# Diagonal of the score tiles by one predicated copy from the third block on, eight buffers for the streamed low halves, and a new table of due times

## The chip, the cores and the metric

The kernel runs on one core of a Trainium2 chip. TensorE (PE) multiplies matrices into eight PSUM banks; VectorE (DVE), ScalarE (ACT) and GpSimd (POOL) work on the elements; SyncE (SP) issues every DMA. Each engine runs its own list of instructions in order, and waits on semaphores of the others. The metric is the device time of one execution in microseconds.

## The reference

Attention with a decaying state comes first, for 4 sequences of 8 heads, 768 steps and head size 48. Its output goes through two feed-forward layers of width 2048 over 3072 tokens of 384 numbers:

```python
for t in range(S):
    state = alpha[:, :, t, :, None] * state + np.einsum('bhd,bhe->bhde', k[:, :, t], v[:, :, t])
    y[:, :, t] = np.einsum('bhd,bhde->bhe', q[:, :, t], state)
...
h = x @ w_in                                  # layer 0
P = a[0] + a[1] * h + a[2] * h2 + a[3] * h3
Q = 1.0 + np.abs(b[0]) * np.abs(h) + np.abs(b[1]) * h2
x = (P / (Q + 1e-06)) @ w_out
...
h = x @ w_in                                  # layer 1
out = (h * np.tanh(softplus(h))) @ w_out
```

The weights arrive as float64 and are taken apart on the chip into a rounded high half and a low half, so that a product is the sum of three.

## The kernel before

**Attention.** The 768 steps are cut into six blocks of 128 (`c`), and the four sequences into two pairs (`b`). `attn_unit(b, c)` does one of the twelve units, number `u = 2 * c + b`. A unit loads its transposed operands (`qka`, SP line 344) and the plain ones (lines 345, 346), and scales them (DVE 358, then two ACT copies into planes, 361). Then it climbs six levels, L = 1 to 32: products on PE (391, 403) give a part of the score tile `AT`, DVE multiplies keys and queries by decays (413, 419), and the planes are written anew (ACT 372, or a DMA at line 370 for u of 4 and more at L = 4 and 8). A level's scores go from PSUM to `AT` by a predicated copy on DVE (441), for L = 32 by four ACT copies (432), and for L = 16 by four ACT copies (438) where `2 * u < N16`. The diagonal of `AT` comes from a sum over `q * k` (DVE 448). Where `2 * u < NDIAG` it is written by 16 ACT instructions, one a head (455), ahead of the first level; otherwise by one predicated copy on DVE (451), behind the level L = 4. Then come the state's outer products (484), the outputs (519, 525) and two transposes (470).

**Feed-forward.** A step is one of 16 slices of 128 hidden units, for one block's 512 tokens: nine products of 128x128x512 into a bank (552), the activation on ACT, DVE and POOL (567 to 589), a split of the result into high (`gh`, 186 or 188) and low half (`gl`, line 179 on DVE or 181 on POOL, as `E_GL` says for each layer and block), and nine products into three banks (601). Sixteen steps make a phase (layer, block), and the order of the phases is `PHASES`. The attention of block c + 1 is due during phase (0, c).

**Weights.** In the first phase of a layer each pair of slices is loaded as float64 and converted (`load_w`: ACT 293, DVE 294, 296, 298, 300, the high half by 186, the low half by 179), and the low halves, with the high halves of the second matrix, are written to DRAM (SP 307, 309). Later phases stream them back (SP 316, 317) into `NWL` and `NWO` buffers in rotation.

**What sets the order.** Nothing is put down in order by hand. Each operation goes to `Plan.add` with an engine, an assumed duration, its dependences and a due time, and `Plan.order` deals them out to the engines: whichever operation is ready goes, the earliest due first. So due times are priorities. `V[i]` is the due time of step i, made of `T0` and of one step length for each phase (`T_PH`); attention units, loads, streams and splits are due at offsets from it. The engines then keep to that list whatever the real durations are, and SP, too, issues in list order: a DMA whose buffer isn't free holds up all DMAs behind it.

Of the kernel before, what the change touches and what calls it, by code (L numbers as in the profile page):

```python
# [31 lines left out]
PE_LV = (0.62, 0.60, 0.58, 0.555, 0.555)  # L32
LEVELS = (1, 2, 4, 8, 16, 32)
NLVM = 5
T0 = 51.78
PHASES = ((0, 0), (0, 1), (1, 0), (0, 2), (1, 1), (0, 3), (1, 2), (0, 4), (1, 3), (0, 5), (1, 4), (1, 5))
T_PH = (8.14, 5.1, 5.16, 5.96, 5.1, 6.27, 4.94, 5.88, 5.4, 4.2, 3.7, 4.1)
D_IN, D_OUT = -3.53, 0.0
AT_P0 = (0.2, -9.467, 0.9)
AT_P1 = (0.45, 0.4, 0.55)  # L40
AT_P = (0.48, 0.447, 0.5)
D_MID = 6.67
LAG = (20.923, 9.487)
D_SPL = (-2.177, 1.881)
W_LEAD, X_LEAD = 4.29, 24.03
D_W1, D_W2 = (36.612, 26.894), (33.033, 27.728)
E_LO = 'VV'
E_TREE, E_QK = ('PPPVPV', 'VVVVVP')
E_M = 'PPVPPV'
E_GL = ('PVPVVV', 'VVVVPP')  # L50
R_PSUM = [0, 0, 0, 0, 0, 0]
NWL, NWO = 6, 8
N16 = 20
NDIAG = 20
NRAW, NF32 = 2, 2
D_Z, D_X, D_EV = 30.2, 5.55, -5.32
N_WARM = 68
D_CST = 5.0
NZ, NG, NU = 4, 3, 3
# [94 lines left out]
def attention_moe_kernel(ctx: ExitStack, tc: tile.TileContext,  # L154
# [166 lines left out]
    def attn_unit(b, c, bf, due):  # L321
# [56 lines left out]
        def level(i, L):  # L378
# [47 lines left out]
            if L == 32:  # L426
                AT2 = AT.rearrange("p (d e) t -> p d e t", d=2)
                for h in range(2):
                    for q in range(2):
# [4 lines left out]
                        act(2 * P, now() + 1, [kb], [kAT], edge)  # L434
            elif L == 16 and 2 * u < N16:
                for h in range(4):
# [10 lines left out]
        def diagonal():  # L447
            dve(2 * DM, now(), [kq, "cst"], [kds], lambda: nc.vector.tensor_reduce(
                out=ds, in_=qn.rearrange("p (h d) -> p h d", h=E2), axis=mybir.AxisListType.X, op=ALU.add), port=False)
            if 2 * u >= NDIAG:  # L450
                dve(W, now(), [kds], [kAT], lambda: nc.vector.copy_predicated(
# [5 lines left out]

        if 2 * u < NDIAG:
            diagonal()
        for i, L in enumerate(LEVELS):  # L460
            level(i, L)
            if L == 4 and 2 * u >= NDIAG:
                diagonal()
# [127 lines left out]
    def split_g(l, r, q, i, due):  # L591
        c = steps[i][1]
        kp, kgh, kgl = f"p{r}", f"gh{q}", f"gl{q}"
        copy(E_GH[l][c], NTOK, due, [kp], [kgh], lambda: ghs[q], lambda: ps[r])
        tt(E_GL[l][c], NTOK, due, [kp, kgh], [kgl],
           lambda: dict(out=gls[q], in0=ps[r], in1=ghs[q].bitcast(F32), op=ALU.subtract))
# [24 lines left out]

    V, t = [], T0
    for n in range(len(PHASES)):
        for f in range(FT):
            V.append(t)
            t += T_PH[n]
    V.append(t)
# [26 lines left out]
    def attend(c):  # L654
        if c == 0:
            t0, t1, p = 0.0, T0, AT_P0
        else:
            t0, t1, p = V[FT * PHASES.index((0, c - 1))], V[FT * PHASES.index((0, c))], AT_P1 if c == 1 else AT_P
        for n in range(2):
# [5 lines left out]
    for i, (l, c, f) in enumerate(steps):  # L665
# [19 lines left out]
        hidden(l, hb, r, i, V[i] + D_MID)  # L685
        split_g(l, r, q, i, V[i] + D_MID + D_SPL[l])
        out_mms(f, q, b, V[i] + LAG[l])
# [86 lines left out]
```

## Time and profile before

| | |
|---|---|
| median of 3 runs | 1068.14 us (1065.29 to 1069.28) |
| the profiled execution: run, and span of its trace | 1065.89 us, 1064.1 us |
| PE busy | 990.3 us, 93% |
| ACT busy | 728.6 us, 68% |
| DVE busy | 694.8 us, 65% |
| POOL busy | 229.4 us, 22% |
| mean granted PE clock | 0.985 |

The first product of the feed-forward (552) starts 78.0 us into the span, and the twelve phases follow. The stretches that are used below run from one phase's first product to the next one's: ahead of the first, then (0, 0), (0, 1), (1, 0), (0, 2), (1, 1), (0, 3), (1, 2), (0, 4) and (1, 3). Averages over the span hide what limits it: the last 200 us hold no attention, and PE is busy in them without a break; in the first 200 us PE waits, and DVE and ACT are nearly always busy.

### The profile page before, as it was taken

The numbers are of one execution on the slowest core, as the hardware profiler recorded it, in microseconds if no ns is written. First come the engines' busy times: TensorE is split into PE (matmuls) and PEld (weight loads), VectorE is DVE, ScalarE is ACT, GpSimd is POOL, SyncE is SP. The second block draws the span as 40 slices with busy tenths as digits, with TensorE's granted clock in tenths as the row PEclk, the third lists the DMA queues.
The fourth block names the chain that finished last, engine by engine and source line by source line (L and its number), as shares of the span: only waits on it lengthen the run. The fifth ranks groups of instructions, "written<-read, shape, count | busy, mean of one in ns | idle before, by whom it ended". The sixth has DMA issues, their size and how long they took to land.

```text
span 1064.1 us, 23681 instructions
## 1 busy us (share of the span) xinstructions
PE 990.3 (93%) x9808; PEld 795.7 (75%) x9808; DVE 694.8 (65%) x937; ACT 728.6 (68%) x1324; POOL 229.4 (22%) x186
## 2 busy tenths in 40 slices
PE   3788879989989999999999999999999999999998
PEld 2566657767777777777877777877878878888887
DVE  8979989888998797763377662359894259700100
ACT  5888969899998898853469874467762269832422
POOL 4014254342310013210112320015310000033232
PEclk9999989899999999999999999999999999999999
DMA  8371546764768855665646556655557345464540
GB/s 319 132 273 45 204 169 216 254 220 125 282 230 289 289 186 149 208 181 167 209 147 174 191 161 190 203 167 158 190 161 219 113 147 149 141 216 142 178 131 30
DMA packets 69483, 195.71 MB, mean 184 GB/s; under 512 B 8064, under 2 KB 28672, under 8 KB 67840
## 3 DMA queue, kind: packets, MB, share of 16 engines
q1 hardware_dynamic: 69376, 194.20, 56.7%
q8 instruction: 77, 1.26, 0.5%
q14 instruction: 30, 0.25, 0.1%
HBM read 157.47 MB, written 28.31 MB: 175 GB/s over the span
## 4 chain that ended last, share of the span: by engine, by line
PE 53%; ACT 18%; DVE 17%; DMA 6%; issue 5%; POOL 1%; SPq 0%; DVEq 0%; ACTq 0%; POOLq 0%
PE bank L601 24%; PE bank L552 22%; DMA Q<-qka 3%; PE bank L525 2%; DVE qka L419 2%; ACT zp L573 2%; ACT u L567 2%; ACT zp L580 2%; ACT Q L372 2%; DVE zp L576 2%; PE bank L519 2%; ACT zp L575 2%; ACT zp L584 1%; PE bank L391 1%; ACT gg L186 1%
## 5 line engine op out<-in xcount | busy, mean ns | idle before, releaser
L601 PE MATMUL bank<-gg,wo 128*128 128x512 f32 x1728 | 436.0, 397 | 4.0 <-ACT gg L186 2.3
L601 PEld LDWEIGHTS bank<-gg,wo 128*128 128x128 f32 x1728 | 322.5, 189 | 74.6 <-ACT gg L186 2.9
L552 PE MATMUL bank<-xh,wih 128*128 128x512 f32 x576 | 230.5, 400 | 11.1 <-DVE zp L578 7.2
L552 PE MATMUL bank<-xl,wih 128*128 128x512 f32 x576 | 225.4, 391 | 2.1 <-DVE xl L546 2.0
L552 PE MATMUL bank<-xh,wl 128*128 128x512 f32 x576 | 225.1, 391 | 0.0
L181 POOL TENSOR_TENSOR gg<-zp,gg 128x512 fp32r<-128x512 f32 x64 | 90.0, 1410 | 413.2 <-ACT gg L186 386.5
L589 ACT ACTIVATE zp<-bank 128x512 f32<-128x512 f32 x96 | 57.1, 598 | 173.6 <-PE bank L552 171.5
L574 POOL TENSOR_TENSOR zp<-zp,u 128x512 f32<-128x512 f32 x64 | 100.5, 1573 | 221.5 <-ACT zp L573 209.6
L552 PEld LDWEIGHTS bank<-xh,wih 128*128 128x128 f32 x576 | 108.2, 188 | 38.1 <-DVE zp L578 7.8
L552 PEld LDWEIGHTS bank<-xl,wih 128*128 128x128 f32 x576 | 108.4, 188 | 24.6 <-DVE xl L546 3.6
L552 PEld LDWEIGHTS bank<-xh,wl 128*128 128x128 f32 x576 | 108.4, 188 | 23.3
L179 DVE TENSOR_TENSOR gg<-zp,gg 128x512 fp32r<-128x512 f32 x128 | 88.9, 700 | 47.0 <-ACT gg L186 45.5
L186 ACT CAST gg<-zp 128x512 fp32r<-128x512 f32 x144 | 88.4, 620 | 18.5 <-DVE zp L585 6.8
L576 DVE SCALAR_TENSOR_TENSOR zp<-zp,sc,bank 128x512 f32<-128x512 f32 x96 | 71.2, 742 | 34.9 <-ACT zp L575 34.7
L585 DVE SCALAR_TENSOR_TENSOR zp<-zp,sc 128x512 f32<-128x512 f32 x96 | 75.9, 799 | 9.8 <-ACT zp L584 8.5
L391 PEld LDWEIGHTS bank<-Q,qka 128*31 128x31 f32 (+4 forms) x3520 | 36.0, 106 | 55.0 <-ACT Q L361 20.1
L580 ACT ACTIVATE zp<-zp,c 128x512 f32<-128x512 f32 x96 | 69.3, 724 | 10.8 <-POOL zp L574 9.2
L391 PE MATMUL bank<-Q,qka 128*31 128x32 f32 (+4 forms) x3520 | 42.1, 199 | 35.4 <-ACT Q L361 14.7
L188 DVE CAST gg<-zp 128x512 fp32r<-128x512 f32 x48 | 24.0, 504 | 74.8 <-ACT zp L589 74.5
L578 DVE SCALAR_TENSOR_TENSOR zp<-zp,sc,bank 128x512 f32<-128x512 f32 x96 | 71.4, 743 | 2.0 <-ACT u L567 0.7
L575 ACT ACTIVATE zp<-bank,sc 128x512 f32<-128x512 f32 x96 | 65.9, 687 | 9.7 <-PE bank L552 9.5
L419 DVE TENSOR_TENSOR qka<-qka,qk 128x1024 f32<-128x1024 f32 x44 | 57.6, 1310 | 19.7 <-PE bank L391 10.1
(108 smaller groups left out, 1174.9 us busy)
## 6 DMA issues: line engine op xcount, KB each, us to landing
wo<-woD SPq DMA_DIRECT2D x160, 384.0 KB, 3.2
wl<-wlD SPq DMA_DIRECT2D x160, 192.0 KB, 2.4
qka<-in_qka_dram SPq DMA_DIRECT2D x11, 1536.0 KB, 6.6
woD<-wo SPq DMA_DIRECT2D x16, 768.0 KB, 4.8
qk<-in_nat_dram SPq DMA_DIRECT2D x11, 768.0 KB, 4.3
Q<-qka SPq DMA_DIRECT2D x32, 256.0 KB, 4.3
raw<-in_w1i_dram SPq DMA_DIRECT2D x8, 768.0 KB, 4.5
wlD<-wl SPq DMA_DIRECT2D x16, 384.0 KB, 3.0
```

Source lines behind the costliest of these rows:

```text
L179: dve(n, due, reads, writes, lambda: nc.vector.tensor_tensor(**kw()))
L181: pool(n, due, reads, writes, lambda: nc.gpsimd.tensor_tensor(**kw()))
L186: act(n, due, reads, writes, lambda: nc.scalar.copy(out=out(), in_=in_()), src="s")
L391: nc.tensor.matmul(lv[o:o + 32 - L, g, :, 16 * z:16 * z + 16].rearrange("p a (n l) -> p a n l", l=L), lhsT=K[:, g * P + o:g * P + o + 32 - L],
L419: dve(W, now(), [kT[L]], [kQC, kK], lambda: nc.vector.tensor_tensor(out=QK, in0=QK, in1=Tv.rearrange("p m x -> p x m").unsqueeze(3).to_bro ...
L552: nc.tensor.matmul(bank[hb], lhsT=w[:, k * P:(k + 1) * P], rhs=x[k], start=(k == 0 and j == 0), stop=(k == KT - 1 and j == 2))
L574: pool(NTOK, due, [ku], [kz], lambda: nc.gpsimd.tensor_tensor(out=zs[r], in0=zs[r], in1=u, op=ALU.mult))
L575: act(NTOK, due, [kh], [kp], lambda: nc.scalar.activation(ps[r], h, AF.Copy, scale=A3), ptr=1)
L576: dve(NTOK, due, [kh], [kp], lambda: nc.vector.scalar_tensor_tensor(out=ps[r], in0=ps[r], scalar=A2, in1=h, op0=ALU.add, op1=ALU.mult), po ...
L580: act(NTOK, due, [], [kz], lambda: nc.scalar.activation(zs[r], zs[r], AF.Ln, bias=c_1), src="s", ptr=1, table="ln")
L585: dve(NTOK, due, [kw], [kp], lambda: nc.vector.scalar_tensor_tensor(out=ps[r], in0=ps[r], scalar=A0, in1=w(), op0=ALU.add, op1=ALU.mult), ...
L601: nc.tensor.matmul(bank[5 + k], lhsT=wos[b][:, w, k * P:(k + 1) * P], rhs=x[q], start=(f == 0 and j == 0), stop=(f == FT - 1 and j == 2))
```

## The change

```diff
-T0 = 51.78
+T0 = 30.44
-T_PH = (8.14, 5.1, 5.16, 5.96, 5.1, 6.27, 4.94, 5.88, 5.4, 4.2, 3.7, 4.1)
+T_PH = (8.22, 4.34, 5.16, 5.96, 5.1, 6.27, 4.94, 5.88, 5.4, 4.2, 4.22, 4.1)
...
-AT_P = (0.48, 0.447, 0.5)
+AT_P = (0.48, 0.487, 0.5)
...
-D_SPL = (-2.177, 1.881)
-W_LEAD, X_LEAD = 4.29, 24.03
+D_SPL = (-2.177, 2.137)
+W_LEAD, X_LEAD = 4.29, 22.42
...
-E_GL = ('PVPVVV', 'VVVVPP')
+E_GL = ('PVPVVV', 'VVPVPP')
...
-NWL, NWO = 6, 8
-N16 = 20
-NDIAG = 20
+NWL, NWO = 8, 8
+N16 = 12
+NDIAG = 8
...
-D_Z, D_X, D_EV = 30.2, 5.55, -5.32
+D_Z, D_X, D_EV = 28.35, 5.55, -5.32
```

`NDIAG` 8 gives the units 4 to 9 (blocks three to five) the predicated copy, which only units 10 and 11 had. `N16` 12 gives units 6 to 9 the predicated copy of the level L = 16. `E_GL` moves the 16 low-half subtractions of phase (1, 2) from DVE to POOL. `NWL` 8 adds two buffers for the streamed low halves. The other numbers are due times. Three places where the lists differ:

SP at the program's start, before; `raw` is a float64 weight load, `qka`, `qk` and `vn` are unit 0's operands, `zp`, `xg` and `u` (shared buffers) hold unit 1's, and `cst` is the table of masks and the identity:

```order
L344 DMA qka_138<-in_qka_dram 128x3072
L345 DMA qk_140<-in_nat_dram 128x1536
L346 DMA vn_139<-in_nat_dram 128x768
L646 DMA cst<-in_consts_dram 128x352
L292 DMA raw_96<-in_w1i_dram 128x768
L344 DMA zp<-in_qka_dram 128x3072
L345 DMA xg<-in_nat_dram 128x1536
L346 DMA u<-in_nat_dram 128x768
L292 DMA raw_96<-in_w1i_dram 128x768
```

And in the changed kernel:

```order
L292 DMA raw_97<-in_w1i_dram 128x768
L344 DMA qka_139<-in_qka_dram 128x3072
L345 DMA qk_141<-in_nat_dram 128x1536
L346 DMA vn_140<-in_nat_dram 128x768
L292 DMA raw_97<-in_w1i_dram 128x768
L307 DMA wlD_93<-wl_85 128x768
L646 DMA cst<-in_consts_dram 128x352
L344 DMA zp<-in_qka_dram 128x3072
L345 DMA xg<-in_nat_dram 128x1536
```

The first weight load now leads, and a second load into the same buffer and a write of the first low half stand ahead of the constants and of unit 1's operands.

DVE in phase (0, 0), where unit 2 ends (506) and unit 3 begins (358), before; `f` is a weight conversion's work tile, and 576 and 578 are the activation of a feed-forward step:

```order
L506 TENSOR_TENSOR S_130<-S_130,bank_114 128x384
L294 TENSOR_SCALAR f_98<-f_98 128x768
L296 TENSOR_SCALAR f_98<-f_98 128x768
L298 SCALAR_TENSOR_TENSOR f_98<-raw_96,f_98 128x768
L300 SCALAR_TENSOR_TENSOR f_98<-raw_96,f_98 128x768
L179 TENSOR_TENSOR wl_85<-f_98,wih_6_75 128x768
L179 TENSOR_TENSOR qk_140<-qk_140 128x768
L448 TENSOR_REDUCE ds_141<-qk_140 128x16
L294 TENSOR_SCALAR f_98<-f_98 128x768
L296 TENSOR_SCALAR f_98<-f_98 128x768
L298 SCALAR_TENSOR_TENSOR f_98<-raw_96,f_98 128x768
L300 SCALAR_TENSOR_TENSOR f_98<-raw_96,f_98 128x768
```

It goes on with `L179` on `wl` and then 358. In the changed kernel:

```order
L506 TENSOR_TENSOR S_131<-S_131,bank_115 128x384
L296 TENSOR_SCALAR f_99<-f_99 128x768
L298 SCALAR_TENSOR_TENSOR f_99<-raw_97,f_99 128x768
L179 TENSOR_TENSOR qk_141<-qk_141 128x768
L300 SCALAR_TENSOR_TENSOR f_99<-raw_97,f_99 128x768
L448 TENSOR_REDUCE ds_142<-qk_141 128x16
L179 TENSOR_TENSOR wl_87<-f_99,wih_6_75 128x768
L358 TENSOR_TENSOR qka_139<-qka_139 128x512
L441 COPY_PREDICATED AT_138<-cst,bank_115 128x512
L576 SCALAR_TENSOR_TENSOR zp<-zp,sc,bank_118 128x512
L578 SCALAR_TENSOR_TENSOR zp<-zp,sc,bank_118 128x512
```

One conversion (294 to 300, 179) has moved from ahead of 358 to behind it, and the copy of unit 3's first level (441) from behind the activations to ahead of them.

Unit 4's diagonal on ACT at the start of phase (0, 1), before; 614 and 575 are feed-forward work:

```order
L455 ACTIVATE AT_137<-cst,ds_141 128x64
L614 COPY u<-bank_119 128x512
L455 ACTIVATE AT_137<-cst,ds_141 128x64 x4
L575 ACTIVATE zp<-bank_117,sc 128x512
L455 ACTIVATE AT_137<-cst,ds_141 128x64 x4
L575 ACTIVATE zp<-bank_118,sc 128x512
L455 ACTIVATE AT_137<-cst,ds_141 128x64 x4
L575 ACTIVATE zp<-bank_116,sc 128x512
L361 COPY Q_136<-qka_138 64x1024
```

In the changed kernel ACT has none of these sixteen (`x4` counts four in a row), and DVE has this:

```order
L441 COPY_PREDICATED AT_138<-cst,bank_116 128x256x2
L300 SCALAR_TENSOR_TENSOR f_100<-raw_98,f_100 128x768
L441 COPY_PREDICATED AT_138<-cst,bank_115 128x128x4
L419 TENSOR_TENSOR qka_139<-qka_139,qk_141 128x2x128x4
L451 COPY_PREDICATED AT_138<-cst,ds_142 128x1024
L585 SCALAR_TENSOR_TENSOR zp<-zp,sc 128x512
```

The diagonal has moved to another engine and from ahead of unit 4's first level to behind its third.

From phase (0, 2) on, PE's list keeps nearly the same places for the attention: of the 384 groups of nine products, counted in thirds, the attention's pieces of units 6 to 11 stand at most four thirds away from where they stood, and those of unit 4 stand up to twelve thirds earlier.

## Rows read from the trace of the kernel before

**Rows 1.** Stretch, us, busy of PE, PEld, DVE, ACT, POOL; clock; DMA.
```profile
0.00:78.00 78.00, 49.78 (x1233) 39.91 (x1233) 66.58 (x82) 58.08 (x128) 15.68 (x26) 0.93 0.66 246
78.00:205.60 127.60, 109.65 (x1258) 86.09 (x1259) 114.85 (x135) 105.98 (x192) 55.25 (x38) 0.93 0.50 177
205.60:284.10 78.50, 74.61 (x795) 59.41 (x793) 69.16 (x95) 75.50 (x141) 25.72 (x21) 1.00 0.62 200
284.10:373.10 89.00, 84.33 (x834) 66.48 (x833) 76.89 (x104) 79.15 (x127) 7.41 (x7) 1.00 0.77 267
373.10:454.40 81.30, 77.34 (x862) 61.71 (x861) 66.31 (x94) 73.86 (x145) 20.11 (x14) 0.98 0.57 178
454.40:538.60 84.20, 81.71 (x770) 66.29 (x768) 39.62 (x61) 35.83 (x76) 5.73 (x8) 1.00 0.63 187
538.60:619.00 80.40, 77.18 (x926) 61.02 (x924) 58.46 (x77) 70.43 (x131) 23.94 (x21) 1.00 0.55 167
619.00:702.30 83.30, 81.47 (x711) 65.75 (x706) 35.37 (x52) 41.97 (x74) 4.04 (x2) 1.00 0.61 189
702.30:779.60 77.30, 75.04 (x830) 59.86 (x828) 68.09 (x98) 59.53 (x101) 28.73 (x16) 1.00 0.56 173
779.60:860.60 81.00, 80.84 (x740) 65.61 (x737) 38.16 (x60) 24.88 (x44) 1.70 (x1) 1.00 0.55 160
```

**Rows 2.** PE's waits from 205.6 to 373: in total, times, longest us.
```profile
PE bank L391 <- ACT Q L361: 1.7, 1, 1.7
PE bank L552 <- ACT zp L589: 1.5, 1, 1.5
```

**Rows 3.** PE's waits from 373 to 538.
```profile
PE bank L391 <- DMA Q<-qka: 2.7, 3, 1.5
PE bank L391 <- ACT Q L372: 2.2, 1, 2.2
```

**Rows 4.** PE's waits from 538 to 702.
```profile
PE bank L391 <- DMA Q<-qka: 2.6, 2, 1.3
```

**Rows 5.** Groups by line, whole span: busy us, mean ns | idle before.
```profile
L181 POOL TENSOR_TENSOR gg<-zp,gg 128x512 fp32r<-128x512 f32 x64 | 90.0, 1410 | 413.2 <-ACT gg L186 386.5 <-issue 16.6 <-PE bank L484 7.2
L179 DVE TENSOR_TENSOR gg<-zp,gg 128x512 fp32r<-128x512 f32 x128 | 88.9, 700 | 47.0 <-ACT gg L186 45.5
...
L441 DVE COPY_PREDICATED AT<-cst,bank 128x512 f32<-128x512 int32 x46 | 46.2, 1004 | 1.1 <-ACT AT L455 0.7 <-PE bank L391 0.2
...
L455 ACT ACTIVATE AT<-cst,ds 128x64 f32<-128x64 f32 x144 | 43.2, 343 | 1.4 <-DVE ds L448 1.3
...
L438 ACT COPY AT<-bank 16x256 f32<-16x256 f32 x36 | 13.1, 363 | 6.5 <-PE bank L391 5.9
...
L451 DVE COPY_PREDICATED AT<-cst,ds 128x1024 f32<-128x1024 int32 x2 | 2.6, 1322 | 0.0
```

**Rows 6.** Timeline near 104 us: start us, us, engine, line, tiles, idle before.
```profile
103.55 1.67 POOL L574 TENSOR_TENSOR zp<-zp,u 128x512 f32<-128x512 f32 x1 [1.82 <-ACT zp L573]
103.99 2.05 DVE L300 SCALAR_TENSOR_TENSOR f<-raw,f 128x768 int32<-128x768 int32 x1
```

**Rows 7.** Timeline from 132 to 142 us: unit 3's load, a conversion, unit 3's start.
```profile
132.34 0.38 SPq L344 DMA_DIRECT2D qka<-in_qka_dram  x1
...
135.88 0.56 DVE L294 TENSOR_SCALAR f<-f 128x768 f32<-128x768 f32 x1 [2.12 <-ACT f L293]
...
137.07 0.96 DVE L298 SCALAR_TENSOR_TENSOR f<-raw,f 128x768 int32<-128x768 int32 x1
...
138.06 0.96 DVE L300 SCALAR_TENSOR_TENSOR f<-raw,f 128x768 int32<-128x768 int32 x1
...
141.10 1.46 DVE L358 TENSOR_TENSOR qka<-qka 128x512 f32<-128x512 f32 x1 [0.22 <-DMA qka<-in_qka_dram]
```

**Rows 8.** Timeline at the start: unit 0's first instruction on DVE.
```profile
9.88 0.69 DVE L358 TENSOR_TENSOR qka<-qka 128x512 f32<-128x512 f32 x1
```

**Rows 9.** DMA issues: tiles, engine, times, KB each, us to landing.
```profile
cst<-in_consts_dram SPq DMA_DIRECT2D x1, 176.0 KB, 8.5
```

## Prediction

> **What bounds the kernel now.** I read the table of busy time by phase first [rows 1], then PE's waits in three stretches [rows 2 to 4], then the groups by line for the prices [rows 5], and last the timeline at two places where the new order moves work [rows 6 to 8].
>
> The table of phases says that there are three regimes. From 0 to 205.6 us DVE is the fullest engine: busy 114.85 of 127.60 us in phase (0, 0), with ACT at 105.98, while PE idles 127.60 - 109.65 = 18.0 us. From 205.6 to 860.6 PE is nearly full: in the eight phases it idles 78.50 - 74.61 = 3.9, then 4.7, 4.0, 2.5, 3.2, 1.8, 2.3 and 0.2 us. After 860.6 there is no attention, and PE decides alone; nothing in the change touches its work there. So what ACT or DVE give up in the middle comes back as time only as far as PE waits for them, and there the 22.6 us of idle is about all that can be won.
>
> The eight phases make four pairs of 32 steps with one block of attention each: (0, 1) with (1, 0) takes 78.5 + 89.0 = 167.5 us, then 165.5, 163.7 and 158.3 [rows 1]. The last pair, with block six, is the one that already has the predicated diagonal and level 16. It also has one state update less, so the differences of 9.2, 7.2 and 5.4 us, together 21.8, bound from above what the other three could win by doing as it does. The first pair has the second layer's weight conversions too, and ACT is busy 154.7 of its 167.5 us.
>
> **The parts of the change.**
>
> *Off ACT.* Six units lose 16 instructions of line 455 each. Their 144 took 43.2 us of busy time, 0.30 each since neighbours overlap [rows 5], so 96 x 0.30 = 28.8 us, 9.6 a block. Four units lose four copies of line 438, 16 x 0.364 = 5.8 us. ACT gives up 34.6 us in all: 9.6 in the pair of block three, 12.5 in each of the next two.
>
> *Onto DVE.* Six copies of line 451 at 1.32 and four of line 441 at 1.00 add 7.9 + 4.0 = 11.9 us. Phase (1, 2) gives back 16 x 0.69 = 11.1 us of subtractions, and POOL takes them at 1.41, 22.6 us [rows 5]. POOL is busy 4.04 of 83.30 us in that phase [rows 1], so this hides; if it didn't, PE would wait 0.7 us a step at most, 11 us. Phase (0, 1) with 69.16 of 78.50 us is the tightest for DVE; it gets 2.6 us.
>
> *What PE gains.* PE's longest waits for ACT are 1.7 + 1.5 us in the first pair [rows 2] and 2.2 in the second [rows 3]; in the third the longest sum is for DMA [rows 4]. The DMA waits, 2.7 and 2.6 us, follow a multiplication on DVE and don't shrink with ACT's load. So the gain lies between 5.4 us (these ACT waits alone) and 21.8 (all three pairs come down to the fourth). I take 4 us in the first pair, 2.5 in the second and 1.5 in the third, 8 in all. That is near the lower end, since the waits are read directly, and the upper end includes conversions and a state update that stay. Should the predicated copies stand in DVE's list where PE waits for DVE, the 11.9 us bound the loss, less the same gain.
>
> A rule of the Trainium skill speaks against the copies, and a row bears on it. Line 300, alone 0.96 us [rows 7], takes 2.05 when it meets a POOL instruction of 1.67 [rows 6]. The page SBUF — State Buffer, section Who interferes with whom, says that a VectorE instruction with two inputs in SBUF contends with a GpSimd instruction that reads SBUF, and that the one that comes second is blocked for the whole of the other. Line 451 reads its mask and its sums from SBUF, so by that rule each copy can be held up. The two copies in the trace took 1.32 on average [rows 5], and show no such hold. Priced from the rows, six copies held as line 300 was, by 1.1 us each, add 6.6 us to DVE; with the same share of it on PE's path as of ACT's waits (5.4 of 34.6) that is 1 us, so the sum stays and the upper range takes it in.
>
> *The start.* DVE now begins with the first weight conversion, two instructions of 0.56 and two of 0.96 [rows 7], 3.0 us ahead of unit 0's first instruction, which was at 9.88 [rows 8] because DVE clears buffers until then. The constants, which unit 0's first products and its diagonal sum need, now stand on SP behind a reload of `raw` that waits for that conversion, so they are issued at about 13 us at the earliest. They took 8.5 us to land in the crowd at the start [rows 9]. So unit 0 begins between 3 us later (conversion alone) and 8.5 + 13 - 11 = 10 us later. But DVE does useful conversions meanwhile, and by the order the conversion work ahead of unit 1's last multiplication is nearly the same as before. DVE was the fuller engine here, 66.58 of 78.00 us [rows 1]. I take +2 for the first feed-forward product, ends 0 and +6.
>
> *Unit 3 in phase (0, 0).* Its load was issued at 132.34 and DVE used it at 141.10 [rows 7]. DVE passed the time with a conversion there; now that conversion stands behind, and DVE waits, then waits again for the first products, since 441 now precedes the activations. That is one conversion and its `wl` subtraction, 3.0 + 1.0 = 4 us, plus some 3 for the wait at 441. On the other side unit 3's first level no longer comes behind three steps' activations, and PE, which waits in this phase for 18.0 us, gets its products sooner. I take -1 for the rest of the phase, ends -8 and +7.
>
> *Eight buffers and earlier streams.* A stream is issued when its buffer's last product is done, so in the new list the first streams wait on PE with other loads behind them. The ones I can follow stand ahead of loads that wait for the same stretch of PE or DVE anyway; I price this at nothing. If that cover is gone, unit 3's load comes a step late, and a step in this phase is 127.6 / 16 = 8.0 us.
>
> **Sum.** +2 - 1 - 8 = -7 us. Against the profiled execution's own run of 1065.9 us that is 1058.9; against the median of 1068.1 it is 1061.1. Runs scatter over 4 us, and I take 1060.
>
> **The rivals.**
>
> *A. ACT is off the path.* Later waits end with DMA and DVE [rows 3, 4], PE's list hardly changes from phase (0, 2) on, and whatever ACT saves becomes ACT's idle time. Then only part of the first pair's 3.2 us comes back: about 1065. For it speaks that ACT is busy only 35.83 of 84.20 and 41.97 of 83.30 us in the second phases of its pairs; against it that it has 75.50 of 78.50 in phase (0, 1).
>
> *B. Slower: the start.* The attention chain, not DVE's load, decides when the first feed-forward product runs. Then unit 0's late constants cost the +6, unit 3's double wait +7, and the pairs give back the first one's 3.2 alone: 1065.9 + 6 + 7 - 3.2 = 1075.7. It decides if the first product of line 552 comes later than about 84 us and phase (0, 0) is not shorter. For it speaks that ACT, too, has its copies behind the diagonal's sums in the new list; against it, that DVE's idle time before 9.88 can't be less than it was, and that it now works on.
>
> *C. Everything comes down to block six.* The three pairs take what the fourth does, -21.8, less the update that stays and the conversions: about -15, with the first 205.6 us unchanged: 1051. For it speaks that the fourth pair has ACT busy 59.53 and 24.88 us where the third has 70.43 and 41.97 [rows 1]; against it that most of PE's idle time there isn't put down to ACT [rows 3, 4].
>
> *D. The change doesn't relieve ACT,* because new table switches or waits fill it. ACT's list has 26 table loads for 24, which is too little for a case of its own.
>
> **How the numbers follow.** Forecast 0.45, with its own range 1053 to 1067; A 0.23; B 0.16; C 0.16. What a measurement of this kernel can tell from no change is about 0.5%, 5.3 us: faster means below 1062.8. The forecast puts three quarters of its chance there, C all of it, A a little: 0.34 + 0.16 + 0.04 = 0.54. Slower, above 1073.5, is most of B and a little of the forecast: 0.14. The rest, 0.32, is the same. The range goes from 1048, inside C, to 1070, inside B.
>
> **What would show it.** ACT busy near 694 us in total and DVE about where it is. The pair of phases (0, 1) and (1, 0) at 163 to 164 us instead of 167.5, the next two at 163 and 162. The first product of line 552 at 80 us, and phase (0, 1) beginning at 206 or 207. If the pairs stay, A is right; if the phases begin later than 212, B; if the pairs reach 158 to 160, C. The prediction is wrong in its mechanism if the time changes by more than 3 us and the pairs have no part in it.

## The result

The changed kernel takes **1073.8 us** (median of 5 runs, 1072.7 to 1076.4), against 1067.9 for the kernel before in runs on the same chip: ratio 1.0073, 95% interval 1.0049 to 1.0098. It is slower, and outside the range of the prediction. The spans of the two profiled runs, 1070.9 and 1064.1 us, show the same difference.

Engine totals of the changed kernel, from its page:

```profile
PE 991.6 (93%) x9808; PEld 793.9 (74%) x9808; DVE 702.6 (66%) x931; ACT 705.2 (66%) x1214; POOL 249.4 (23%) x202
```

The page of before has ACT at 728.6, DVE at 694.8 and POOL at 229.4. So ACT gave up 23.4 us, DVE got 7.8 and POOL 20.0: the work moved as the change says. The groups by line of the changed kernel (busy us, mean ns, idle before), which answer to [rows 5]:

```profile
L181 POOL TENSOR_TENSOR gg<-zp,gg 128x512 fp32r<-128x512 f32 x80 | 113.9, 1426 | 458.2 <-ACT gg L186 428.0 <-issue 14.3 <-DMA qka<-in_qka_dram 5.9
...
L441 DVE COPY_PREDICATED AT<-cst,bank 128x512 f32<-128x512 int32 x50 | 49.1, 982 | 13.8 <-PE bank L391 8.7 <-ACT gg L186 4.1 <-ACT AT L455 1.0
...
L455 ACT ACTIVATE AT<-cst,ds 128x64 f32<-128x64 f32 x48 | 13.8, 343 | 2.7 <-DMA cst<-in_consts_dram 2.5
...
L451 DVE COPY_PREDICATED AT<-cst,ds 128x1024 f32<-128x1024 int32 x8 | 12.7, 1593 | 0.0
```

Line 455 fell from 43.2 to 13.8 us and the copy of line 451 rose from 2 to 8. Busy time by phase of the changed kernel, with the columns of [rows 1]; a phase runs from the first product of line 552 in its first step to that of the next phase:

```profile
0.00:80.80 80.80, 49.79 (x1232) 39.46 (x1232) 68.28 (x83) 58.37 (x128) 12.44 (x26) 0.98 0.66 243
80.80:204.90 124.10, 106.56 (x1257) 82.86 (x1255) 109.35 (x128) 103.73 (x188) 50.28 (x37) 0.96 0.47 162
204.90:289.90 85.00, 75.68 (x787) 59.75 (x787) 77.66 (x100) 71.18 (x123) 28.66 (x22) 0.96 0.64 203
289.90:383.00 93.10, 87.83 (x842) 69.54 (x842) 80.70 (x107) 81.08 (x114) 9.57 (x8) 0.98 0.76 269
383.00:463.30 80.30, 76.69 (x862) 60.36 (x861) 67.83 (x93) 69.13 (x119) 19.76 (x14) 1.00 0.57 176
463.30:547.10 83.80, 81.76 (x770) 66.33 (x769) 41.64 (x64) 28.53 (x49) 5.51 (x8) 1.00 0.63 187
547.10:626.80 79.70, 78.05 (x929) 61.42 (x927) 61.12 (x81) 67.80 (x117) 24.89 (x21) 1.00 0.56 169
626.80:709.10 82.30, 80.72 (x702) 65.16 (x703) 29.28 (x36) 37.55 (x64) 25.38 (x18) 1.00 0.61 190
```

Row for row against [rows 1]: the start +2.8 us, phase (0, 0) -3.5, then (0, 1) +6.5 and (1, 0) +4.1, so the first pair +10.6; the second pair -1.5, the third -1.7; nothing behind. Rounding apart, the sum is the 6.8 us between the spans. The start and phase (0, 0) together come to -0.7, so **the loss shows up in phases (0, 1) and (1, 0)**. PE is idle for 85.00 - 75.68 = 9.3 us and 5.3 us in the two, where before it was 3.9 and 4.7. Its waits there, in the changed kernel (in total, times, longest), first from 204.9 to 289.9 us, then to 383:

```profile
PE bank L391 <- ACT Q L372: 3.2, 1, 3.2
PE bank L552 <- DVE xl L546: 1.8, 1, 1.8
PE bank L484 <- DVE S L492: 1.3, 1, 1.3
```

```profile
PE bank L552 <- DVE xl L546: 3.3, 2, 2.6
```

Before, no wait there was longer than 1.7 us [rows 2]. Behind each of the two long ones the granted clock is at half. In the changed kernel's windows around them (the columns are those of the phases) the clock is 0.60 and 0.79:

```profile
218.00:226.50 8.50, 5.29 (x76) 4.05 (x75) 7.95 (x9) 6.53 (x11) 2.83 (x2) 0.60 0.82 268
290.00:298.00 8.00, 4.70 (x12) 3.22 (x13) 7.96 (x9) 7.35 (x13) 2.27 (x2) 0.79 0.60 220
```

So the profile offers several causes for the same stretch: PE waits for ACT and DVE, the clock behind the waits, and DVE, which is busy for 7.95 of 8.50 and 7.96 of 8.00 us there. DVE's busy time rose by 77.66 - 69.16 = 8.5 us in phase (0, 1) and by 3.8 in (1, 0).

### The profile page after: what moved, and what is told of

It reads as the page before. It is cut to its first block, busy times and chain, and to the rows that moved or that the text cites. A ratio compares the mean times of both kernels' runs of the same rounds, so it can differ in the third digit from the quotient of the medians.

```text
span 1070.9 us, 23609 instructions
## 1 busy us (share of the span) xinstructions
PE 991.6 (93%) x9808; PEld 793.9 (74%) x9808; DVE 702.6 (66%) x931; ACT 705.2 (66%) x1214; POOL 249.4 (23%) x202
## 4 chain that ended last, share of the span: by engine, by line
PE 48%; DVE 22%; ACT 18%; DMA 5%; issue 5%; POOL 1%; SPq 0%; DVEq 0%; ACTq 0%; POOLq 0%
PE bank L601 22%; PE bank L552 21%; DVE zp L585 3%; DMA Q<-qka 3%; DVE qka L419 2%; DVE zp L576 2%; ACT zp L580 2%; DMA qka<-in_qka_dram 2%; ACT zp L575 2%; DVE zp L578 2%; ACT Q L372 2%; ACT gg L186 2%; ACT zp L584 2%; DVE AT L441 2%; ACT zp L573 2%
## 5 line engine op out<-in xcount | busy, mean ns | idle before, releaser
L601 PEld LDWEIGHTS bank<-gg,wo 128*128 128x128 f32 x1728 | 319.3, 188 | 74.3 <-DVE gg L179 3.9
L181 POOL TENSOR_TENSOR gg<-zp,gg 128x512 fp32r<-128x512 f32 x80 | 113.9, 1426 | 458.2 <-ACT gg L186 428.0
L585 DVE SCALAR_TENSOR_TENSOR zp<-zp,sc 128x512 f32<-128x512 f32 x96 | 79.7, 834 | 10.9 <-ACT zp L584 9.7
L179 DVE TENSOR_TENSOR gg<-zp,gg 128x512 fp32r<-128x512 f32 x112 | 80.1, 718 | 10.4 <-ACT gg L186 9.0
L419 DVE TENSOR_TENSOR qka<-qka,qk 128x1024 f32<-128x1024 f32 x44 | 57.0, 1295 | 19.4 <-PE bank L391 10.6
```

The lines of the kernel that those rows point to most:

```text
L179: dve(n, due, reads, writes, lambda: nc.vector.tensor_tensor(**kw()))
L181: pool(n, due, reads, writes, lambda: nc.gpsimd.tensor_tensor(**kw()))
L419: dve(W, now(), [kT[L]], [kQC, kK], lambda: nc.vector.tensor_tensor(out=QK, in0=QK, in1=Tv.rearrange("p m x -> p x m").unsqueeze(3).to_bro ...
L585: dve(NTOK, due, [kw], [kp], lambda: nc.vector.scalar_tensor_tensor(out=ps[r], in0=ps[r], scalar=A0, in1=w(), op0=ALU.add, op1=ALU.mult), ...
L601: nc.tensor.matmul(bank[5 + k], lhsT=wos[b][:, w, k * P:(k + 1) * P], rhs=x[q], start=(f == 0 and j == 0), stop=(f == FT - 1 and j == 2))
```

## The experiments

Two theories stood at first. **C**: the predicated copies on DVE make the loss. **D**: the new order of the lists makes it, which the due times and the eight buffers bring. Each run is given by its ratio to the kernel before on the same chip, and by the phases of its one profiled execution, from the start times of line 552's products. The first pair is (0, 1) with (1, 0), the second and third are the next two; "end" is where the first pair ends.

```
                        start  (0,0)  (0,1)  (1,0)  pair 1   end    pair 2  pair 3   ratio
before                   78.0  127.6   78.4   89.0   167.4   373.1   165.5   163.7   1
changed                  80.8  124.1   85.0   93.1   178.1   383.0   164.0   162.0   1.0073
copies_alone             78.0  127.2   80.1   88.9   168.9   374.2   166.5   162.7   0.9992
dues_alone               81.2  124.2   83.0   96.8   179.8   385.1   168.0   167.0   1.0138
copies_from_block4       81.0  124.0   82.8   96.7   179.5   384.5   164.1   162.4   1.0074
step_5p1                 80.9  123.6   88.9   93.7   182.6   387.1   165.9   162.1   1.0111
before_buf8              77.6  123.0   84.3   97.2   181.5   382.1   160.8   165.8   1.0053
after_buf6               80.7  127.1   84.0   92.2   176.2   384.0   165.5   162.1   1.0097
step15_first             81.1  130.1   80.6   95.0   175.6   386.8   164.6   162.1   1.0101
both_waits               81.2  131.0   79.8   94.5   174.3   386.6   163.7   161.0   1.0094
filled_waits             82.1  125.0   86.2   91.4   177.6   384.7   163.2   167.0   1.0097
old_first                79.3  126.7   80.1   88.9   169.0   375.0   168.3   160.2   1.0015
old_first_block4         78.1  127.2   78.4   88.8   167.2   372.5   164.9   162.5   0.9991
old_to_step16            78.4  128.1   81.3   93.2   174.5   381.0   164.5   162.1   1.0042
new_to_step16            82.2  131.7   82.5   88.9   171.4   385.4   167.4   163.2   1.0111
old_to_step32            77.4  127.9   80.1   92.1   172.2   377.5   164.9   160.8   0.9993
old16_moved              77.4  127.6   81.1   93.3   174.3   379.3   163.2   163.1   1.0042
old16_moved_xl           78.0  126.6   84.7   93.7   178.4   383.0   163.6   161.3   1.0044
old_to_step32_block4     79.3  127.2   78.5   94.8   173.3   379.8   164.7   162.1   1.0018
```

The intervals of the ratios reach 0.0017 to 0.0036 to either side. A single phase differs by 1 to 2 us between profiles of programs that are alike there (the start of the changed order lies between 80.7 and 82.2).

### The copies or the table

The kernel before with the copies alone:

```diff
-N16 = 20
-NDIAG = 20
+N16 = 12
+NDIAG = 8
```

> The kernel before with N16 12 and NDIAG 8 and nothing else: the predicated copies with the old due times and the old six buffers. The changed kernel lost 10.6 us in the pair of phases (0, 1) and (1, 0) (167.5 us before, 178.1 after). Theory D, that the due table did it by dealing unit 4's work out ahead of the first steps' activations: this pair takes 163 to 167 us, and the kernel 1058 to 1064. Theory C, that the copies on DVE did it (1.3 us each, and held up by POOL): the pair takes 172 us or more, and the kernel 1069 or more.

And the changed kernel without them, so the due times, the buffers and `E_GL` alone:

```diff
-N16 = 12
-NDIAG = 8
+N16 = 20
+NDIAG = 20
```

> The changed kernel with N16 20 and NDIAG 20: the new due times, the eight buffers and the subtractions on POOL, with the diagonal and the level L = 16 on ACT as before. Theory D: the pair of phases (0, 1) and (1, 0) takes 175 us or more, and the kernel 1073 or more, since ACT has its 34.6 us again. Theory C: the pair takes 165 to 170 us, and the kernel 1063 to 1069.

The copies alone do nothing: 1065.75 us, ratio 0.9992 (0.9976 to 1.0009). The rest alone costs 14.3 us: 1081.06 us, 1.0138 (1.0108 to 1.0168). Theory C falls. Theory D's own forecast for the copies alone, 1058 to 1064, is missed too: in the old order they win nothing that can be told from noise. Beside the new table the kernel with the copies is faster than the one without, 1.0073 against 1.0138, some 7 us. By the two profiles it is 11.2, of which 4.0 and 5.0 lie in the second and third pair, where the old order gives 1.0 us away and wins 1.0. So what a moved instruction is worth depends on the list it is moved in; the planner deals the list out anew for each of these kernels, so this compares whole lists.

Two single numbers were tried next, the third block's copy and one due time, in the changed kernel:

```diff
-NDIAG = 8
+NDIAG = 12
```

> The changed kernel with NDIAG 12: only the third block's two diagonals go back to ACT, 32 instructions. Theory C, the copy at unit 4 as the cause: the pair takes 167 to 172 us, and the kernel 1062 to 1067. Theory D: the pair stays at 176 or more, the kernel at 1071 or more.

```diff
-T_PH = (8.22, 4.34, 5.16, 5.96, 5.1, 6.27, 4.94, 5.88, 5.4, 4.2, 4.22, 4.1)
+T_PH = (8.22, 5.1, 5.16, 5.96, 5.1, 6.27, 4.94, 5.88, 5.4, 4.2, 4.22, 4.1)
```

> The changed kernel with the step length of phase (0, 1) in the due table back at 5.1 us from 4.34. Theory D, in the form that this number packs attention and activations of that phase together: the pair takes 166 to 171 us, and the kernel 1061 to 1066. Theory C: the pair stays at 176 or more.

Neither is the cause. Without the third block's copy the time is 1074.56 us, the same as with it. The due time of before makes 1078.63 us, and a pair of 182.6: a miss for that form of theory D.

### The eight buffers

> The kernel before with eight buffers in place of six, the rest as before. Theory D, eight buffers: the second layer's first conversion moves up to the end of step 15 as in the changed kernel, and the pair goes from 167.4 to 172 to 178 us, total 1071 to 1077. Theory D, due times, and theory C: within 2 us of 1066.8, pair 166 to 169.

> The changed kernel with six buffers for the streamed low halves in place of eight, the rest as changed; the planner sets the lists anew. Theory D in the form that the eight buffers made the bad order: the second layer's first conversion goes back to behind the end of step 15 (in the list of ACT it stands 57 places behind it, where it stands 4 behind in the changed kernel), phase (0, 1) at 79 to 81, pair at 168 to 172, total 1064 to 1068. In the form that the due times alone made it: pair 176 to 180, total 1071 to 1075. Theory C: the same as that.

The edits are `NWL` from 6 to 8 in the kernel before and from 8 to 6 in the changed one. Eight buffers alone cost the kernel before 1.0053 (1.0032 to 1.0075), with a pair of 181.5; but six in the changed kernel bring nothing back, 1.0097 (1.0061 to 1.0133). So no one number is the cause: the eight buffers with the old table, and the new table (with the copies) with six buffers, each give an order with a first pair of 176 us or more.

### Taking the waits away

The finished list of a kernel can be edited behind the planner, so long as every operation stays behind those it depends on. The first two edits go after PE's two long waits. In the changed kernel the last activation of step 15 ends late. Line 585 of that step on DVE, in the timeline of the kernel before and of the changed one (start us, us):

```profile
197.92 1.37 DVE L585 SCALAR_TENSOR_TENSOR zp<-zp,sc 128x512 f32<-128x512 f32 x1
```

```profile
205.88 0.74 DVE L585 SCALAR_TENSOR_TENSOR zp<-zp,sc 128x512 f32<-128x512 f32 x1
```

It stands behind the second layer's first conversions, and behind it come step 15's output group, the evacuation of block 0 and, by way of the shared `u` buffers, the first activations of phase (0, 1). ACT has copies of unit 4's Q ahead of those as well, in the timeline of the changed kernel:

```profile
218.61 0.58 ACT L614 COPY u<-bank 128x512 f32<-128x512 f32 x1 [2.45 <-PE bank L601]
220.48 1.26 ACT L372 COPY Q<-qka 64x512 f32<-64x512 f32 x2 [1.28 <-DVE qka L419]
221.76 0.60 ACT L567 ACTIVATE u<-bank 128x512 f32<-128x512 f32 x1
```

`step15_first` moves the end of step 15 up; `both_waits` moves the activations of steps 16 and 17 and the differences of x for phase (1, 0) as well, with three more entries of the same kind (the numbers are those of the operations in the planner):

```diff
+MOVES = [([801], 757), ([805, 806], 1275), ([807], 1276), ([808], 395), ([809], 395), ([810, 811, 812], 959), ([813, 814], 830), ([815, 816], 830), ([817, 818], 830)]
...
+        for moved, ahead_of in MOVES:
+            out = [n for n in out if n not in moved]
+            i = out.index(ahead_of)
+            out[i:i] = moved
         return [(ops[n][4], ops[n][7]) for n in out]
```

> The changed kernel with its own table, copies and buffers; in the finished lists only the end of step 15 is moved up: POOL's 574 of step 15 ahead of its subtractions gl1 and gl2, ACT's 580 and 584 of step 15 ahead of the second layer's first conversion, DVE's 585 of step 15 ahead of line 294 of that conversion, gh0 and gl0 behind them, PE's three products of the last output group ahead of step 16's first product, and the three evacuations with their stores ahead of the column copies of Q. Theory D (the order of the lists makes the loss, here the late end of step 15): phase (0, 1), 85.0 us in the changed kernel, comes to 79 to 82, its PE wait of 3.2 us at the products of level 4 to under 1, the total 3 to 6 us lower, 1068 to 1071. Theory C (the copies on DVE make it): no copy is moved, so within 1 us of 1073.8, pair 178.

> As the kernel with step 15 first, and besides ACT's first activations of steps 16 and 17 ahead of the first two copies of unit 4's Q columns, PE's products of step 19 ahead of those of level 4, and at the start of phase (1, 0) the rounding and the differences of x (lines 186, 546) ahead of the subtraction gl2 of step 30. Theory D: both long PE waits of the pair (3.2 us for ACT at level 4, 2.6 us for DVE at the first product of phase (1, 0)) go, and with them the stretches at half clock behind them: pair (0, 1) with (1, 0) from 178.1 to 168 to 172 us, total 1064 to 1068. Theory C: 1073.8, pair 178.

Both missed: 1078.39 and 1077.54 us, no better than the changed kernel. Phase (0, 1) is shorter by 4.4 and 5.2 us, as expected, but phase (0, 0) is longer by 6.0 and 6.9. Much of both is the boundary alone, since the end of step 15 now stands ahead of it. PE's waits from 200 to 300 us with step 15 first (line numbers are shifted by 5 here):

```profile
PE bank L475 <- ACT vn L537: 3.6, 1, 3.6
PE bank L396 <- ACT Q L377: 3.5, 1, 3.5
```

A wait for ACT at a copy of `vn` has come ahead of the phase's boundary, and the one at the levels is as long as it was.

The third edit asks for the price of the clock. PE gets products whose results are overwritten, in its two long waits:

```diff
+FILL = {846: (5, 8), 1292: (4, 6)}
...
+    for emit, table, n in plan.order():
+        to, count = FILL.get(n, (0, 0))
+        for _ in range(count):
+            nc.tensor.matmul(bank[to][:, 0:2 * P], lhsT=ident, rhs=cst[:, 0:2 * P], start=True, stop=True)
```

> The changed kernel, and PE has work in its two long waits: eight products of 256 columns (0.44 us by the planner's figure) ahead of level 4 of unit 4, where it waited 3.2 us for ACT and then ran at a granted clock of half for some 4 us, and six ahead of the first product of step 32, where it waited 2.6 us for DVE and did the same; their results are overwritten. If half of the loss is the clock after those waits: both stretches at full clock, phases (0, 1) and (1, 0) from 85.0 and 93.1 to 82 to 84 and 90 to 92 us, total 1069 to 1071. If the clock there costs nothing (other engines set the pace): within 1 us of 1073.8.

The windows of this kernel around the same two places:

```profile
218.00:226.50 8.50, 7.79 (x157) 6.24 (x156) 8.14 (x10) 4.69 (x9) 1.09 (x1) 1.00 0.80 247
...
290.00:298.00 8.00, 6.95 (x33) 5.30 (x32) 7.96 (x10) 7.97 (x15) 3.35 (x2) 1.00 0.70 257
```

The clock is 1.00 where it was 0.60 and 0.79, and the nine products behind level 4 take 2.4 us where they took 3.9. Yet the pair takes 177.6 us for 178.1, where 2 to 6 us less were expected of the clock: phase (1, 0) falls by 1.7 us, to 91.4 and into its forecast, but (0, 1) rises by 1.2. So **the half clock is not what makes the loss**; a price of 1 to 2 us can't be told from the scatter of single profiles. DVE is busy for 8.14 of 8.50 and 7.96 of 8.00 us at the two places. The total, 1076.83 us (1.0097, 1.0071 to 1.0122), is no lower either; its profile has 5 us more in phase (1, 2), where PE waits 3.5 us at once for a DMA, and why that came is open.

### The order itself

If the order is the cause, the old order must bring the time back with everything else as changed. Both tables give the same operations with the same numbers, so the list can begin with the old order and go on with the changed one. `FIRST` holds the numbers of the first 1578 operations, up to step 48's first product, in the order of the run with the copies alone:

```diff
+        first = json.loads(zlib.decompress(base64.b85decode(FIRST)))
+        taken = set(first)
+        out = first + [n for n in out if n not in taken]
         return [(ops[n][4], ops[n][7]) for n in out]
```

> The changed kernel with its copies, its eight buffers and its table, but the first 1578 operations of its finished list, those up to step 48's first product (the end of phase (1, 0)), stand in the order that the table of before gives with the same copies (the list of the run with the copies alone); from there on the order of the changed kernel. Theory D in its last form (the loss is in the order alone, between the start and the end of phase (1, 0)): pair (0, 1) with (1, 0) at 167 to 170 us in place of 178.1, the next two pairs as in the changed kernel, 164 and 162, total 1061 to 1064. The rival that eight buffers or the copies cost by themselves, whatever the order: pair 174 to 180, total 1069 to 1075.

> As the one with the old order first, and the predicated copies start with block four, so that block three keeps its 16 small copies a unit on ACT. Theory D: pair (0, 1) with (1, 0) at 166 to 169 us, next pairs 164 and 162, total 1060 to 1063, within 2 us of the one with the old order first. The rival that the third block's copy was worth having even in the old order: 1 to 3 us slower than that one.

The first pair comes to 169.0 and 167.2 us. Busy time of its two phases with the old order first, to be held against [rows 1] and the changed kernel's:

```profile
206.00:286.00 80.00, 75.67 (x794) 59.09 (x793) 71.07 (x95) 69.98 (x122) 24.68 (x21) 1.00 0.60 194
286.00:375.00 89.00, 84.36 (x834) 66.32 (x834) 79.16 (x105) 78.53 (x110) 7.43 (x7) 1.00 0.77 271
```

With the copies and eight buffers, the pair is within 1.6 us of before. **Theory D holds in the form that the order alone makes the loss**; the buffers and the copies together, in the old order, cost nothing that can be told from noise. The totals, 1069.46 us (1.0015, 0.9996 to 1.0035) and 1065.28 (0.9991, 0.9973 to 1.0008), cannot be told from before. Both are above what was expected, 1061 to 1064 and 1060 to 1063: the gain of the later pairs did not add in the first of them, where pair 2 takes 168.3 us and pair 3 160.2. The second, with the third block's diagonals on ACT, is 4.2 us faster than the first, where within 2 was expected; the two intervals overlap, and the same edit gains nothing in the list with the old order up to step 32, below.

Then the list was cut elsewhere: the old order up to step 16 and up to step 32, and the reverse, the changed order up to step 16 and the old one behind.

> The changed kernel, with the old order for the first 842 operations of the list, up to step 16's first product (start and phase (0, 0)), and the changed order behind. If what stands ahead of step 16 makes the loss (the late end of step 15, with the conversions that stand beside it): pair (0, 1) with (1, 0) 168 to 172 us, phase (0, 0) near 127, total 1062 to 1067. If the order inside the pair makes it: pair 174 to 180, total 1071 to 1077.

> The changed kernel, with the old order for the first 1231 operations, up to step 32's first product (start, phases (0, 0) and (0, 1)), and the changed order behind. If the loss lies ahead of step 32: pair 167 to 171 us, of which phase (0, 1) 79 to 82. If it lies in phase (1, 0): phase (0, 1) 79 to 82 and phase (1, 0) 93 to 97, pair 173 to 178.

> The reverse: the changed order for the start and phase (0, 0), the old order from step 16's first product to step 48's, the changed order behind. If what stands ahead of step 16 makes the loss: pair 174 to 180 us, total 1070 to 1076. If the order inside the pair makes it: pair 167 to 172, total 1062 to 1068, with phase (0, 0) at 124 as in the changed kernel.

With the old order up to step 32 the loss is gone (1066.88 us, 0.9993, 0.9978 to 1.0009), though phase (1, 0) still takes 92.1 us: those 3 us come back in the next two pairs, which take 164.9 + 160.8 = 325.7 us for the 328.5 with the old order first. The pair's 172.2 us fall between the two forecasts, and it is the total that decides: what counts lies **ahead of step 32**. With the old order up to step 16 alone, 1071.62 us (1.0042, 1.0023 to 1.0062): a part is back, and some 4.7 us stay in the order of phase (0, 1). The reverse is worst, 1079.10 us (1.0111), outside both forecasts, with a phase (0, 0) of 131.7 us for 124.1:

```profile
82.20:214.00 131.80, 108.74 (x1261) 84.11 (x1260) 116.25 (x136) 106.28 (x191) 54.72 (x38) 0.94 0.47 165
```

This one shows a debt that the phase table hides. In the changed order the first products of step 16 stand ahead of step 15's output group, so phase (0, 1) "begins" at 204.9 us although step 15 is late by 8 us. With the old order behind, step 16 must wait for step 15's group, and the debt stands where it arises: phase (0, 1) begins at 214.0, 8.4 us later than before, of which 4.2 are the later start and 4.1 a longer phase (0, 0). The two parts do not add up: the changed start makes the old pair end 10.4 us later (385.4 against 375.0) and the changed pair 2.0 later (383.0 against 381.0).

The last three edits try for the rest inside the pair: in the list with the old order up to step 16, the output group of step 15, the evacuation and the activations of steps 16 and 17 moved up as in the runs above (`old16_moved`), then the differences of x too (`old16_moved_xl`), and, for a better version, the old order up to step 32 with copies from block four on. The edit is again a `FIRST`, with the rows moved in the first two and `NDIAG` 12 in the third.

> As the one with the old order up to step 16 (1071.6 us, phase (0, 1) 81.3), and at the head of phase (0, 1): PE's three products of step 15's output group ahead of step 16's first product, the three evacuations of block 0 with their stores ahead of the column copies of Q, ACT's activations of steps 16 and 17 ahead of the first two diagonal copies of unit 4's Q, and PE's products of step 19 ahead of level 4. If these rows are the loss inside the pair: PE's 3.2 us wait at level 4 and the half clock behind it go, phase (0, 1) 76 to 79, pair 169 to 172, total 1066 to 1069. If the loss there is spread over the engines: pair 173 to 176, total 1070 to 1073.

> As the one before, and the rounding and the differences of x for phase (1, 0) ahead of the subtraction gl2 of step 30. If PE's 2.6 us wait at step 32's first products is on the path: 2 to 3 us less than the one before, pair 167 to 170, total 1064 to 1067. If it is not: within 1 us of it.

> The old order up to step 32, the changed one behind, predicated copies from block four on. If the order up to step 32 holds the whole loss and the third block's copies are worth 1 us the wrong way in that order: total 1063 to 1066, at or a little below before (1067 to 1068).

They give 1071.36 (1.0042), 1071.13 (1.0044) and 1067.16 us (1.0018, 0.9999 to 1.0037). The third is above its forecast and no faster than with the third block's copies (1066.88). The moves bring nothing: in the first of them PE still waits as long at level 4, and ACT behind DVE. The waits of PE from 200 to 300 us, then of ACT from 204 to 226, where line numbers are shifted by 31:

```profile
PE bank L422 <- ACT Q L403: 3.1, 1, 3.1
```

```profile
ACT Q L403 <- DVE qka L450: 2.7, 1, 2.7
```

Line 450 here is the 419 of the changed kernel, DVE's multiplication for unit 4's next level. It took 2.29 us, where the median of its group in the changed kernel is 1.22. No version beats the kernel before.

**What the chain of work shows.** The profile's chain of the work that ended last tells which engine sets the pace. In phase (0, 1) of the kernel before it runs through PE for 42 us, ACT for 19 and DVE for 4; in the changed kernel through PE for 1, ACT for 38 and DVE for 37. With the old order first it is 6, 42 and 24. Pieces of the chain (start us, us; each counts from the end of the one before), in the kernel before and then in the changed one:

```profile
205.78 6.13 PE bank L552 x27
...
225.90 4.31 PE bank L601 x18
```

```profile
221.79 1.12 PE bank L391 x64
222.93 0.74 DVE AT L441
223.67 1.98 DVE qka L419
225.65 2.34 DVE AT L451
227.99 1.68 DVE zp L585
```

The last three are stretched (the median of line 419's group is 1.22 us, of 451's 1.32 and of 585's 0.75), beside work of POOL that is shown further down. Over the phase, DVE instructions on the chain that took 0.2 us or more above the median of their group add up to 4.7 us in the changed kernel, to none before, to 1.0 with the old order first and to 2.7 with the old order up to step 16. It is no measure of the loss in every run: with both waits moved it is 1.4.

**What stays open:** which rows of phase (0, 1) hold the 4.7 us that the cuts at steps 16 and 32 differ by, and by what mechanism. The waits that the moves aimed at stayed, or others came in their place, which speaks against a single wait. The chain speaks for DVE, and for its meetings with POOL in particular, but no run took work off DVE or POOL there in the same order to show it. Without the third block's copies, in a list dealt anew, phase (0, 1) was 2.2 us shorter and (1, 0) 3.6 longer.

## Why the prediction was wrong

**The pair (0, 1) with (1, 0), "4 us in the first pair": the step that failed.** A gain of 4 us was forecast, and the pair came out 10.6 us longer. The argument priced what ACT gives up against PE's waits for ACT of before [rows 2], as if the waits of the new list were the old ones less ACT's relief. But a due time changes where every operation stands in the lists of in-order engines, and the waits of the changed kernel are new ones: 3.2 us for ACT at level 4, and for DVE at line 546 3.3 us in phase (1, 0), where the trace of before has 1.3. It also took phase (0, 1) for PE's, "nearly full", and gave DVE 2.6 us more there; DVE's busy time rose by 8.5, and the chain of work went over to DVE and ACT. The run with the copies alone did what that argument is about, ACT's relief in nearly the old order, and it gained nothing: the pair went from 167.4 to 168.9, the total to 0.9992. So even its lower bound of 5.4 us for the three pairs was too high, and as far as the copies go rival A, "ACT is off the path", was right. ACT itself was relieved as forecast by line (455 by 29.6 us over all its forms, 438 by 5.8); its total fell by only 23.4, to 705 instead of 694, since two more table loads took 2.6 and the small copies had partly overlapped other records, which a total counts once.

**"Eight buffers and earlier streams ... I price this at nothing."** This failed with it. In the old order eight buffers cost nothing that can be told from noise, but the order that they bring cost the kernel before 4.8 us. The cover named for that price was the loads that wait anyway; that the planner deals out the rows of all engines anew had no term.

**The start, "+2", ends 0 and +6:** +2.8. Right, and the reason holds as far as the trace shows it: DVE's first conversion comes at once after the clearing, ahead of unit 0 [rows 8], whose line 358 follows 3.0 us later:

```profile
9.88 0.55 DVE L294 TENSOR_SCALAR f<-f 128x768 f32<-128x768 f32 x1
...
12.93 0.68 DVE L358 TENSOR_TENSOR qka<-qka 128x512 f32<-128x512 f32 x1
```

The constants were worse off than that sum had them, and it cost no more: they took 5.0 us to land instead of the 8.5 of [rows 9], but were issued at 15.9 us, not 13, and landed at 20.9, 9.8 us later than before. (The prediction's late end for unit 0, 8.5 + 13 - 11, is 10.5 and not 10.)

**The rest of phase (0, 0), "-1", ends -8 and +7:** -3.5 by the phase's boundary, inside the ends, and yet wrong in what it stands for. DVE's two waits at unit 3, forecast at 4 and 3 us, came (DVE's waits from 80.8 to 204.9 us in the changed kernel: in total, times, longest):

```profile
DVE qka L358 <- DMA qka<-in_qka_dram: 4.2, 1, 4.2
DVE AT L441 <- ACT gg L186: 4.1, 1, 4.1
```

But the last activation of step 15 starts 8.0 us later on DVE. The boundary moved ahead of work that was still owed. Where the old order behind made the phase pay it, in the reverse cut, phase (0, 0) was 4.1 us longer than before and not 3.5 shorter.

**The second and third pair, "2.5" and "1.5":** -1.5 and -1.7, near in size for the third and 1.0 short for the second. The reason is in doubt: with the old order the copies give these pairs +1.0 and -1.0, and a part of the gain in the changed kernel is work moved out of phase (1, 0), as the cut at step 32 shows.

**Rival B, slower by the start, 1075.7,** came nearest in time, but for another reason. Its sign, a first product of line 552 later than 84 us, did not show (80.8). The loss came from the rows up to step 31 as a whole, not from unit 0's constants. So its nearness is luck. The range ended at 1070 since outside the start and unit 3 no case had a new order that makes waits of its own, and none had a first pair that grows, though the words on what is queued behind a late stream were there.

**The rule on VectorE and GpSimd** (the Trainium skill, SBUF — State Buffer, section Who interferes with whom) was weighed at 1 us, with the remark that the two copies of before show no hold. After the change it shows. The timeline of DVE, then of POOL, in the changed kernel:

```profile
223.56 2.08 DVE L419 TENSOR_TENSOR qka<-qka,qk 128x1024 f32<-128x1024 f32 x1
225.57 2.42 DVE L451 COPY_PREDICATED AT<-cst,ds 128x1024 f32<-128x1024 int32 x1
227.88 1.77 DVE L585 SCALAR_TENSOR_TENSOR zp<-zp,sc 128x512 f32<-128x512 f32 x1
```

```profile
223.28 1.28 POOL L574 TENSOR_TENSOR zp<-zp,u 128x512 f32<-128x512 f32 x1 [8.18 <-ACT zp L573]
224.95 4.15 POOL L574 TENSOR_TENSOR zp<-zp,u 128x512 f32<-128x512 f32 x2 [0.38 <-ACT zp L573]
```

The copy of line 451 takes 2.42 us where its median is 1.32, and the two around it are 0.9 and 1.0 us over theirs, all beside POOL's line 574, of which the last two took 4.15 us where one has a median of 1.33. The trace agrees with that page of the Trainium skill. Two of the eight copies were held, 2.2 us in all, for the six and 6.6 us of the estimate. But the estimate looked at the copies alone. Summed over phase (0, 1), DVE's instructions stand 8.2 us above the medians of their groups in the changed kernel and 2.1 in the one before, nearly all of it in instructions that overlap one of POOL's (7.7 and 2.0); with the old order first it is 3.9. So the order also sets how often the two engines meet. Over all runs this sum goes with the result: it is 2.0 to 3.9 us in the six kernels of a ratio up to 1.002, and 5.3 to 9.0 in those of 1.004 and more, but for the reverse cut (4.0), whose loss stands ahead of that phase. Whether it makes the loss or only marks it, no run shows.

## What to carry to other kernels

A number that steers a list scheduler is not a local edit: price it as a new order, with waits of its own, and leave the range open to the slower side. To find out whether the order is to blame, run the new operations in the old order, and cut the list at several points, before any single wait is chased; aiming at waits that the profile names brought nothing here in five runs. And a phase's boundary is only a measure if the same work lies ahead of it in both kernels.

## What was not expected of the hardware

The granted clock fell to half behind PE waits of 3.2 and 2.6 us, and keeping PE busy held it at 1.00, with the pair of phases only 0.5 us shorter, while DVE was busy nearly throughout. POOL's instructions stretch too when they meet DVE's: a subtraction of line 181 of 1.29 us (median) took 4.51 us at 207.4 us in the changed kernel, while DVE ran without a pause beside it. DVE's instructions up to 210.8 us there read two tensors from SBUF each, the next one reads a tensor and a PSUM bank, and the subtraction ended at 211.9, 1.1 us after the last of the former. That looks like one hold through several instructions on end.
